# A decode block's load queue in written order, its row loads moved and cut, its last weight loads cut finer, and fewer warm matmuls

## The chip, the cores and the metric

The kernel runs on one core of one Trainium2 chip. The metric is device time in microseconds (us) of one execution. A profiled execution has a span (first to last instruction), and its own time is a little longer.

The engines are TensorE (PE; its weight loads are listed as PEld), VectorE (DVE), ScalarE (ACT), GpSimd (POOL) and SyncE (SP). SyncE and ScalarE each have a DMA queue here. All DMAs run on the core's 16 DMA engines.

## What is computed

A pre-norm attention block with a KV cache, one token for each of 4 batch entries, then a channel MLP. All data are float32.

```python
x = A_x                                             # (4, 1, 448)
y = layernorm(x)
q = (y @ wq)                                        # 16 heads of 256
k, v = last 1024 positions of the caches            # 8 kv heads, 2 q heads each
p = softmax(q k^T * 256 ** -0.5);  o = p v
h = x + o @ wo
z = layernorm(layernorm(h))
out = h + gelu(z @ w1 + b1) @ w2 + b2               # 448 -> 1792 -> 448
```

The caches, cut to their last 1024 positions, and the weights are 88 MB, each byte read once.

## The kernel before

**Groups.** The 8 kv heads are 8 groups, numbered 0 to 7. For each group the kernel projects `q` (`project_q`: matmuls `pq`, a copy `qs` on ScalarE, four transposes `pqt`, DVE work into `qT`), computes scores in two halves of 512 positions (`scores_half`: 8 matmuls `s`, a maximum `mx` on DVE), the softmax (`softmax`: DVE's `nm`, two exponentials `p` on ScalarE, row sums and `rec`), transposes the exponentials (`transpose_p`: `ppt`, then DVE copies into `pT`), multiplies with the values (`values`: 16 matmuls into `po`), and adds the group's output (`finish`: DVE's `o`, transposes `pot`, DVE's `oT`, matmuls `acc` with the group's `wo`). Four matmuls with 32 rows each go to the four column groups of the TensorE array, one per batch entry or per quarter of the work.

**Loads.** Three big buffers of the pool `ring` are filled in turn (`slot`). The first, `t`, gets `wq` for group 0, the keys of group 0 (`k0`) and part of `wq` for group 1; the rest of that comes by two small transfers into `wq1_last`. Then each load is one DMA of 7,040 or 7,936 KB: `ta`, `tb`, `tc`, `td` for g = 0, and again for g = 3, which bring keys, values and weights of three groups packed by the host in the order of their use. The end (`te0` to `te2`, one in each of the three buffers) holds the keys of group 7, values and `wo` of groups 6 and 7, and the MLP weights `w1` and `w2`, in 11 DMAs. A load into a buffer waits until the last reader of what was in it is done.

**Rows.** `rs` holds three row blocks that the MLP part at the end needs: `xb` (the input), `b2b` and `b1b` (biases), four partitions for each quarter of the array. GpSimd clears it, and ScalarE issues four DMAs (line 127) that fill it.

**Order.** TensorE runs in written order (`manual_schedule`); the other engines' instructions are put in order by a scheduler from the written one and the dependencies. DMAs on hardware queues take eight completion counters in turn; a DMA that takes one over waits until the DMA that had it before has landed.

**The end.** After the scores of group 7, `keep_warm` puts bf16 matmuls on a zero tile `idle` between TensorE's work: 2 ahead of `transpose_p` for group 7, 10 behind it, and one to three at later places. Then come the values of group 6 and 7, interleaved with the output of group 6; the sum `last` of all outputs in a layout of four quarters; the residual and two layer norms (`h`, `dh`, `z`, `pz`); `pu` (with `w1`), the GELU `u`, its transpose `put` into `gT`; and the second MLP product, of 14 chunks of 128 rows: `pa` takes chunks 0 to 7, is copied by ScalarE to `pas` and added in, and `py` takes chunks 8 to 13. DVE adds the residual (`res`) and SyncE stores it.

Of the kernel before, what the change touches and what calls it, by code (L numbers as in the profile page):

```python
# [15 lines left out]
B, D = 4, 448  # L16
# [4 lines left out]
P = 128  # L21
# [3 lines left out]
NFC = F // P  # L25
FQ = F // 4
Q = 32
CACHE = NKC * B * DH
# [7 lines left out]
def block_kernel(ctx: ExitStack, tc, rows, wq0, k0, wq1, la, lb, lc, ld, k7, vo, w1, w2, out):  # L36
    nc = tc.nc
# [12 lines left out]
    def slot(name):  # L50
        return ring.tile([P, SLOT], F32, tag="r", name=name)

    def load(t, at, src, pieces=None):
        dst = t[:, at : at + src.shape[-1]]
        at = 0
        for n in pieces or (src.shape[-1],):
            nc.sync.dma_start(dst[:, at : at + n], src[:, at : at + n])
            at += n
        return dst

    def cut(t, sizes):
        parts, at = [], 0
        for n in sizes:
            parts.append(t[:, at : at + n])
            at += n
        return parts


    def wq_parts(t, last=None):
        parts = [(a, yT[:, a, :], slice(0, 512), t[:, a * 512 : (a + 1) * 512]) for a in range(3)]  # L70
        if last is not None:
            return parts + [(3, yT[:H, 3, :], slice(0, 512), last)]
        for i in range(2):
            parts.append((3, yT[:, 3 + i, :], slice(i * 2 * P, (i + 1) * 2 * P), t[:, 3 * 512 :]))
        return parts


    def keys(t):
        return t.rearrange("p (c b k) -> p c b k", c=2, b=B)

    def chunks(t):
        v = t.rearrange("p (c b d) -> p c b d", b=B, d=DH)
        return [v[:, c : c + 2] for c in range(0, v.shape[1], 2)]
# [18 lines left out]
    yT = const.tile([P, ND + 1, Q], F32, name="yT")  # L102
# [20 lines left out]

    rs = const.tile([P, 2 * P + FQ], F32, name="rs")
    nc.gpsimd.memset(rs, 0.0)
    for j in range(4):
        nc.scalar.dma_start(rs[j * Q : j * Q + B, :], rows[j])
    xb, b2b, b1b = rs[:, :P], rs[:, P : 2 * P], rs[:, 2 * P :]


# [20 lines left out]
    def project_q(g, parts):  # L151
        pq = ps_m.tile([P, 512], F32, tag="m", name=f"pq{g}")
        for j, y, cols, w in parts:
            nc.tensor.matmul(pq[j * Q : (j + 1) * Q, cols], y, w, start=True, stop=True)  # L154
        qs = work.tile([P, 512], F32, tag="qs", name=f"qs{g}")
        nc.scalar.copy(qs, pq)  # L156

        pt = ps_m.tile([P, 2 * REP, P], F32, tag="m", name=f"pqt{g}")
        for i in range(2 * REP):
            nc.tensor.transpose(pt[:, i, :], qs[:, i * P : (i + 1) * P], ident)  # L160
        sm = work.tile([P, 2 * REP, B], F32, tag="sm", name=f"sm{g}")
        nc.vector.tensor_reduce(  # L162
            sm, pt.rearrange("p i (j q) -> p i q j", j=4)[:, :, :B, :], axis=AX.X, op=ALU.add
        )

        src = sm.rearrange("p (r c) b -> p c b r", r=REP)
        for i in range(2):
            nc.vector.tensor_copy(qT[g % 2][:, :, :, i * REP : (i + 1) * REP], src)

    def scores_half(g, h, kt):  # L170
        s = ps_s.tile([P, 512], F32, tag="s", name=f"s{g}_{h}")
        for c in range(2):
            for b in range(B):
                nc.tensor.matmul(  # L174
                    s[b * Q : (b + 1) * Q, :], qT[g % 2][:, c, b, :], kt[:, c, b, :],
                    start=(c == 0), stop=(c == 1),
                )
        m = work.tile([P, 1], F32, tag=f"mx{h}", name=f"mx{g}_{h}")
        nc.vector.reduce_max(m, s, axis=AX.X)  # L179
        return s, m  # L180

    def softmax(g, parts):
        halves, mx = zip(*parts)
        nm = work.tile([P, 1], F32, tag="nm", name=f"nm{g}")
        nc.vector.tensor_max(nm, mx[0], mx[1])
        nc.vector.tensor_scalar_mul(nm, nm, -SCALE)  # L186
        p = once.tile([P, 2 * 512], F32, tag="p", name=f"p{g}")
        sums = work.tile([P, 2], F32, tag="sums", name=f"sums{g}")
        for h in range(2):
            nc.scalar.activation(  # L190
                p[:, h * 512 : (h + 1) * 512], halves[h], AF.Exp, bias=nm, scale=SCALE,
                accum_out=sums[:, h : h + 1],
            )
        rec = work.tile([P, 1], F32, tag=f"rec{g % 3}", name=f"rec{g}")
        nc.vector.tensor_add(rec, sums[:, 0:1], sums[:, 1:2])
        nc.vector.reciprocal(rec, rec)
        return p, rec

    def scores(g, kt):
        return softmax(g, [scores_half(g, h, kt[h]) for h in range(2)])  # L200

    def transpose_p(g, p):
        for h in range(2):
            pt = ps_t.tile([P, 4, P], F32, tag="t", name=f"ppt{g}_{h}")
            for c in range(4):
                nc.tensor.transpose(pt[:, c, :], p[:, (4 * h + c) * P : (4 * h + c + 1) * P], ident)  # L206

            src = pt.rearrange("p (c i) (b q) -> p c i b q", i=2, b=B)
            for i in range(2):
                nc.vector.tensor_copy(  # L210
                    pT[g % 2][:, 2 * h : 2 * h + 2, :, i * REP : (i + 1) * REP], src[:, :, i, :, :REP]
                )


    def values(g, vt, po, pairs=range(NKC // 2)):
        for c in pairs:
            for b in range(B):
                nc.tensor.matmul(  # L218
                    po[b * Q : (b + 1) * Q], pT[g % 2][:, c, b, :], vt[c][:, :, b, :],
                    start=(c == 0), stop=(c == NKC // 2 - 1),  # L220
                )
# [35 lines left out]
    def po_tile(g, pool=ps_o, tag="o"):  # L257
        return pool.tile([P, 2, DH], F32, tag=tag, name=f"po{g}")
# [6 lines left out]
    ka, kb, wqt1 = cut(load(t, WEIGHTS + ND * B, k0), (HALF, HALF, 3 * 512))  # L265
# [12 lines left out]
    nc.vector.tensor_mul(yT[H:, 4, :B], d[H:, 3, :], rx[H:, :])  # L278
    project_q(0, wqt)

    p, rec = scores(0, [keys(ka), keys(kb)])
    project_q(1, wq_parts(wqt1, wq1_last))
    transpose_p(0, p)

    def finish(g, po, rec, wt):
        transposed_output(g, po, rec)
        add_output(g, output_weights(wt))

    for g in (0, 3):
        ka, kb, wqt, va = cut(load(slot(f"ta{g}"), 0, la[g // 3]), (HALF, HALF, WEIGHTS, HALF))  # L290
        p, rec_next = scores(g + 1, [keys(ka), keys(kb)])
        project_q(g + 2, wq_parts(wqt))
        transpose_p(g + 1, p)
        po = po_tile(g)
        va = chunks(va)
        values(g, va, po, range(0, 2))

        vb, wot, ka, kb = cut(load(slot(f"tb{g}"), 0, lb[g // 3]), (HALF, WEIGHTS, HALF, HALF))
        values(g, va + chunks(vb), po, range(2, 4))
        p, rec_then = scores(g + 2, [keys(ka), keys(kb)])  # L300
        finish(g, po, rec, wot)
        transpose_p(g + 2, p)

        wqt, v, wot, ka = cut(load(slot(f"tc{g}"), 0, lc[g // 3]), (WEIGHTS, CACHE, WEIGHTS, HALF))
        project_q(g + 3, wq_parts(wqt))
        po = po_tile(g + 1)
        values(g + 1, chunks(v), po)
        first_half = scores_half(g + 3, 0, keys(ka))
        finish(g + 1, po, rec_next, wot)

        kb, wqt, v, wot = cut(load(slot(f"td{g}"), 0, ld[g // 3]), (HALF, WEIGHTS, CACHE, WEIGHTS))
        p, rec = softmax(g + 3, [first_half, scores_half(g + 3, 1, keys(kb))])
        project_q(g + 4, wq_parts(wqt))
        transpose_p(g + 3, p)
        po = po_tile(g + 2)
        values(g + 2, chunks(v), po)
        finish(g + 2, po, rec_then, wot)


    g = HKV - 2  # L320
    e = [slot(f"te{i}") for i in range(3)]
    kt = [keys(t) for t in cut(load(e[0], 0, k7), (HALF, HALF))]
# [2 lines left out]
    vt_last = chunks(load(e[2], 0, vo[1][:, :CACHE], (CACHE // 4, CACHE // 2, CACHE // 4)))  # L325
    wo_last = output_weights(load(e[1], CACHE + WEIGHTS, vo[1][:, CACHE:]))
    w1t = cut(load(e[0], CACHE, w1, (2 * F, F + F // 2)), (F, F, F, F // 2))
    w2t = cut(load(e[2], CACHE, w2, (8 * D, 4 * D, 2 * D)), NFC * (D,))
    p, rec_last = scores(g + 1, kt)


    warm0 = ps_o.tile([P, 512], F32, tag="o", name="warm0")

    def keep_warm(n, warm):
        for _ in range(n):
            nc.tensor.matmul(warm[:Q], idle[:, :Q], idle, start=True, stop=True)  # L336

    keep_warm(2, warm0)
    transpose_p(g + 1, p)
    keep_warm(10, warm0)  # L340
    po = po_tile(g)
    values(g, vt, po)
    po_last = po_tile(g + 1, ps_t, "t")
# [17 lines left out]
    for i in range(4):  # L361
        for j in range(4):
            nc.tensor.matmul(
                ph[j * Q : (j + 1) * Q], oT[(g + 1) % 2][:, i, :], columns(wo_last[:, i, :], j),
                start=False, stop=(i == 3),
# [18 lines left out]
    h = once.tile([P, P], F32, tag="h", name="h")  # L384
# [27 lines left out]
    for a in range(ND):  # L412
        m = Q if a == 0 else B
        for j in range(4):
            rows, w = w1_part(a, j)
# [31 lines left out]
    for c in range(first):  # L447
        j, m = c % 4, Q if c < 4 else B
# [6 lines left out]
    for c in range(first, NFC):  # L455
        for j in range(4):
            m, n = (Q, 2) if c == first else (B, 2 if j < 3 else 1)
# [80 lines left out]
```

## Time and profile before

| | us |
|---|---|
| median of 3 executions | 215.76 |
| lowest, highest of the 3 | 214.77, 216.06 |
| profiled execution: its own time | 214.81 |
| its span | 213.0 |

In the profile's 40 slices each digit is a busy share in tenths. A row of the chain of waits has a start, a length and what the time went to; "x16" counts instructions. In a row of instruction groups, "out<-in" are the program's names without numbers, and a matmul on float32 data leaves two records. A bracket at the end of a timeline row gives the idle time of the engine before the row and what ended it. The mean granted clock of TensorE was 0.848 of full speed.

### The profile page before, as it was taken

How to read it: one execution, taken by the hardware profiler on the slowest of the kernel's cores; microseconds unless marked ns; L12 is line 12 of the kernel's file. 1: busy time of each engine (PE TensorE's matmuls, PEld its weight loads, DVE VectorE, ACT ScalarE, POOL GpSimd, SP SyncE). 2: the span in 40 equal slices, each digit the busy share in tenths (PEclk: the TensorE clock that was granted, in tenths of full speed). 3: DMA queues.
4: the chain of work that ended last, by engine and by line, in shares of the span. 5: the costliest groups of instructions: out<-in, count | busy, mean ns of one | idle time of the engine just before them, and what ended most of it. 6: DMA issues, size and time to landing. Idle time of an engine off the chain costs nothing.

```text
span 213.0 us, 2294 instructions
## 1 busy us (share of the span) xinstructions
PE 137.4 (64%) x971; PEld 48.2 (23%) x971; DVE 38.4 (18%) x167; ACT 21.2 (10%) x52; POOL 5.6 (3%) x17
## 2 busy tenths in 40 slices
PE   0456824872970595289398198239809876998993
PEld 0322211220220221023123022113202322334432
DVE  1420320320230012012114013100301223122320
ACT  0210110120020100021003001000000302000310
POOL 6100000000000000000000000000000000000110
PEclk9999995796697579769859959955965999999999
DMA  7999899999999999999999999999999998999990
GB/s 291 433 392 502 381 486 391 447 467 409 417 453 444 417 417 477 390 465 391 458 423 444 425 456 417 429 417 465 405 410 415 430 450 380 435 414 435 420 376 34
DMA packets 3289, 88.46 MB, mean 415 GB/s; under 512 B 384, under 2 KB 512, under 8 KB 1104
## 3 DMA queue, kind: packets, MB, share of 16 engines
q1 hardware_dynamic: 3248, 88.29, 96.7%
q8 instruction: 7, 0.11, 0.2%
q10 hardware_dynamic: 32, 0.05, 0.1%
q14 instruction: 2, 0.02, 0.0%
HBM read 88.26 MB, written 0.07 MB: 415 GB/s over the span
## 4 chain that ended last, share of the span: by engine, by line
DMA 64%; PE 29%; DVE 3%; ACT 1%; issue 1%; SPq 0%; ACTq 0%; DVEq 0%
DMA ta<-la 21%; DMA td<-ld 20%; DMA tb<-lb 16%; PE s L174 8%; DMA t<-k 8%; PE po L218 8%; PE ppt L206 2%; PE pu L416 2%; PE warm L336 1%; PE acc L247 1%; PE pq L154 1%; PE pot L239 1%; PE pa L449 1%; DVE o L235 1%; DVE mx L179 1%
## 5 line engine op out<-in xcount | busy, mean ns | idle before, releaser
L179 DVE TENSOR_REDUCE mx<-s 128x1 f32<-128x512 f32 x16 | 11.1, 691 | 61.0 <-PE s L174 61.0
L174 PE MATMUL s<-ta,qT 128*32 128x512 f32 x64 | 12.2, 935 | 8.9 <-DMA ta<-la 8.9
L156 ACT COPY qs<-pq 128x512 f32<-128x512 f32 x8 | 4.7, 585 | 112.3 <-PE pq L154 112.3
L190 ACT ACTIVATE p<-s,nm 128x512 f32<-128x512 f32 x16 | 10.9, 687 | 45.9 <-DVE nm L186 45.9
L174 PE MATMUL s<-td,qT 128*32 128x512 f32 x32 | 7.3, 1061 | 12.0 <-DMA td<-ld 12.0
L235 DVE TENSOR_SCALAR o<-po,rec 128x512 f32<-128x512 f32 x8 | 6.0, 751 | 47.1 <-PE po L218 47.1
L218 PE MATMUL po<-tb,pT 128*32 128x512 f32 x32 | 7.3, 1061 | 10.4 <-DMA tb<-lb 10.4
L154 PE MATMUL pq<-tc,yT 128*32 128x512 f32 (+1 forms) x20 | 3.9, 890 | 14.8 <-DMA tc<-lc 14.8
L206 PE MATMUL ppt<-ident,p 128*128 128x128 f32 x64 | 10.5, 286 | 2.0 <-ACT p L190 1.7
L218 PE MATMUL po<-tc,pT 128*32 128x512 f32 x64 | 10.5, 815 | 0.0
L160 PE MATMUL pqt<-ident,qs 128*128 128x128 f32 x32 | 6.6, 341 | 6.0 <-ACT qs L156 6.0
L174 PE MATMUL s<-tb,qT 128*32 128x512 f32 x64 | 9.1, 717 | 0.0
L206 PEld LDWEIGHTS ppt<-ident,p 128*128 128x128 f32 x64 | 6.7, 140 | 7.1 <-ACT p L190 7.1
L218 PE MATMUL po<-te,pT 128*32 128x512 f32 x64 | 7.9, 596 | 0.1
L162 DVE TENSOR_REDUCE sm<-pqt 128x16 f32<-128x64 f32 x8 | 1.8, 224 | 33.9 <-PE pqt L160 33.9
L174 PE MATMUL s<-t,qT 128*32 128x512 f32 x32 | 6.1, 925 | 2.6 <-DMA t<-k 2.6
L218 PE MATMUL po<-td,pT 128*32 128x512 f32 x64 | 7.3, 595 | 0.0
L336 PE MATMUL warm<-idle 128*32 128x512 bf16 x25 | 7.3, 382 | 0.0
L160 PEld LDWEIGHTS pqt<-ident,qs 128*128 128x128 f32 x32 | 4.2, 169 | 12.1 <-ACT qs L156 10.3
L174 PEld LDWEIGHTS s<-ta,qT 128*32 128x32 f32 x64 | 2.9, 163 | 17.4 <-issue 14.4
L239 PE MATMUL pot<-ident,o 128*128 128x128 f32 x32 | 5.2, 287 | 2.2 <-DVE o L235 2.2
L148 POOL TENSOR_TENSOR r<-ve_r,mhalf 128x1 f32<-128x1 f32 x2 | 1.1, 542 | 192.2 <-DVE ve_r L147 192.2
(129 smaller groups left out, 113.4 us busy)
## 6 DMA issues: line engine op xcount, KB each, us to landing
tc<-lc SPq DMA_DIRECT2D x2, 7936.0 KB
td<-ld SPq DMA_DIRECT2D x2, 7936.0 KB
ta<-la SPq DMA_DIRECT2D x2, 7040.0 KB, 29.4
tb<-lb SPq DMA_DIRECT2D x2, 7040.0 KB, 34.3
te<-vo SPq DMA_DIRECT2D x1, 4992.0 KB, 27.2
t<-k SPq DMA_DIRECT2D x1, 4864.0 KB, 16.4
te<-k SPq DMA_DIRECT2D x1, 4096.0 KB, 36.9
te<-w SPq DMA_DIRECT2D x2, 1792.0 KB, 28.0
```

Source lines behind the costliest of these rows:

```text
L154: nc.tensor.matmul(pq[j * Q : (j + 1) * Q, cols], y, w, start=True, stop=True)
L156: nc.scalar.copy(qs, pq)
L160: nc.tensor.transpose(pt[:, i, :], qs[:, i * P : (i + 1) * P], ident)
L174: nc.tensor.matmul(s[b * Q : (b + 1) * Q, :], qT[g % 2][:, c, b, :], kt[:, c, b, :], start=(c == 0), stop=(c == 1),)
L179: nc.vector.reduce_max(m, s, axis=AX.X)
L190: nc.scalar.activation(p[:, h * 512 : (h + 1) * 512], halves[h], AF.Exp, bias=nm, scale=SCALE, accum_out=sums[:, h : h + 1],)
L206: nc.tensor.transpose(pt[:, c, :], p[:, (4 * h + c) * P : (4 * h + c + 1) * P], ident)
L218: nc.tensor.matmul(po[b * Q : (b + 1) * Q], pT[g % 2][:, c, b, :], vt[c][:, :, b, :], start=(c == 0), stop=(c == NKC // 2 - 1),)
L235: nc.vector.tensor_scalar_mul(o, po, rec)
L239: nc.tensor.transpose(pt[:, i, c], o[:, i, c * P : (c + 1) * P], ident)
L336: nc.tensor.matmul(warm[:Q], idle[:, :Q], idle, start=True, stop=True)
L416: nc.tensor.matmul(pu[j * Q : j * Q + m, :], zT[rows, a, :m], w, start=(a == 0), stop=(a == ND - 1),)
```

## The change

Four things are changed.

1. SyncE and ScalarE are added to the engines that run in written order. So that ScalarE's written order suits, `scores` no longer contains the softmax; it is called where wanted, behind the next group's `project_q`.
2. The four row transfers at the start are taken out. Rows are loaded by seven: four behind the load of `tb` for g = 0 (two quarters, each cut into columns 0 to 255 and 256 to 703), three behind that of `td` (one quarter cut the same way, one whole).
3. The last weights `w2` come in loads of 8, 3, 2 and 1 chunks, where it was 8, 4 and 2.
4. Around `transpose_p` of group 7, the 2 and 10 warm matmuls become two `fill` matmuls (float32, on real data, output unused) and 2 warm ones.

```diff
-    for j in range(4):
-        nc.scalar.dma_start(rs[j * Q : j * Q + B, :], rows[j])
...
     def scores(g, kt):
-        return softmax(g, [scores_half(g, h, kt[h]) for h in range(2)])
+        return [scores_half(g, h, kt[h]) for h in range(2)]
...
-        p, rec_next = scores(g + 1, [keys(ka), keys(kb)])
+        parts = scores(g + 1, [keys(ka), keys(kb)])
         project_q(g + 2, wq_parts(wqt))
+        p, rec_next = softmax(g + 1, parts)
         transpose_p(g + 1, p)
...
         vb, wot, ka, kb = cut(load(slot(f"tb{g}"), 0, lb[g // 3]), (HALF, WEIGHTS, HALF, HALF))
+        if g == 0:
+            for j in range(2):
+                for cols in (slice(0, 2 * P), slice(2 * P, 2 * P + FQ)):
+                    nc.scalar.dma_start(rs[j * Q : j * Q + B, cols], rows[j][:, cols])
...
         kb, wqt, v, wot = cut(load(slot(f"td{g}"), 0, ld[g // 3]), (HALF, WEIGHTS, CACHE, WEIGHTS))
-        p, rec = softmax(g + 3, [first_half, scores_half(g + 3, 1, keys(kb))])
+        if g == 0:
+            for j in range(2, 4):
+                for cols in ((slice(0, 2 * P), slice(2 * P, 2 * P + FQ)) if j < 3 else (slice(0, 2 * P + FQ),)):
+                    nc.scalar.dma_start(rs[j * Q : j * Q + B, cols], rows[j][:, cols])
+        parts = [first_half, scores_half(g + 3, 1, keys(kb))]
         project_q(g + 4, wq_parts(wqt))
+        p, rec = softmax(g + 3, parts)
...
-    w2t = cut(load(e[2], CACHE, w2, (8 * D, 4 * D, 2 * D)), NFC * (D,))
-    p, rec_last = scores(g + 1, kt)
+    w2t = cut(load(e[2], CACHE, w2, (8 * D, 3 * D, 2 * D, D)), NFC * (D,))
+    p, rec_last = softmax(g + 1, scores(g + 1, kt))
...
+    def fill(n):
+        for _ in range(n):
+            nc.tensor.matmul(warm0[:Q], yT[:, 0, :], kt[0][:, 0, 0, :], start=True, stop=True)
+
+    fill(2)
+    transpose_p(g + 1, p)
     keep_warm(2, warm0)
-    transpose_p(g + 1, p)
-    keep_warm(10, warm0)
...
-        with tc.manual_schedule(engines={mybir.EngineType.PE}):
+        with tc.manual_schedule(engines={mybir.EngineType.PE, mybir.EngineType.SP, mybir.EngineType.Activation}):
```

SyncE's queue at the start, before. `t`, `ta`, `tb`, `tc` are the first buffers, `wq`, `k`, `la`, `lb`, `lc` their inputs; the bracket names what the DMA waits for, DMAHWn being completion counter n.

```order
L57 DMA t_134<-wq 128x1808
L57 DMA t_134<-k 128x9728
L267 DMA wq_last<-wq 32x1x512 x2
L57 DMA ta_239<-la 128x14080 [waits DMAHW0_49]
L57 DMA tb_313<-lb 128x14080 [waits DMAHW1_49]
L57 DMA tc_382<-lc 128x15872 [waits DMAHW2_49,DVE_49,PE_49]
```

The same place in the changed kernel.

```order
L57 DMA t_130<-wq 128x1808
L57 DMA t_130<-k 128x9728
L265 DMA wq_last<-wq 32x1x512 x2
L57 DMA ta_235<-la 128x14080
L57 DMA tb_309<-lb 128x14080
L57 DMA tc_382<-lc 128x15872 [waits DMAHW1_49,DMAHW0_49,DMAHW2_49,DVE_49,PE_49]
```

The loads stand in the same sequence; the waits of the first `ta` and `tb` for the counters of `wq` and `k` are gone.

ScalarE's queue in the changed kernel, from the exponentials of group 1 (`p_279`) to those of group 2 (`p_348`).

```order
L188 ACTIVATE p_279,sums_280<-s_0_237,nm_276 128x512 [waits DVE_49,Activation_49]
L188 ACTIVATE p_279,sums_280<-s_1_248,nm_276 128x512
L302 DMA rs<-rows 4x256 [waits Pool_49]
L302 DMA rs<-rows 4x448
L302 DMA rs<-rows 4x256 [waits DMAHW0_49]
L302 DMA rs<-rows 4x448 [waits DMAHW1_49]
L188 ACTIVATE p_348,sums_349<-s_0_323,nm_345 128x512 [waits DVE_49,PE_49,Activation_49]
```

Before, the four row transfers stood ahead of everything on ScalarE. The other three now stand between the copies `qs` of groups 3 and 4.

TensorE around the last scores, before: `s_1` is the second half of the scores of group 7, `warm` what `keep_warm` writes, `ppt` the transposes of group 7's exponentials, `po_886` the values of group 6. Of the warm matmuls one is shown at each of the two places.

```order
L174 MATMUL s_1_838<-te_813,qT_112 32x512 x8
L336 LDWEIGHTS idle
L336 MATMUL warm_859<-idle 32x512
...
L206 MATMUL ppt_0_862<-ident,p_852 128x128 x4
L206 MATMUL ppt_1_869<-ident,p_852 128x128 x4
...
L218 MATMUL po_886<-te_814,pT_113 32x512 x16
```

The same place in the changed kernel, with the first of two warm matmuls.

```order
L172 MATMUL s_1_842<-te_816,qT_112 32x512 x8
L349 MATMUL warm_863<-te_816,yT 32x512 x2
L204 MATMUL ppt_0_866<-ident,p_856 128x128 x4
L204 MATMUL ppt_1_873<-ident,p_856 128x128 x4
L345 LDWEIGHTS idle
L345 MATMUL warm_863<-idle 32x512
...
L216 MATMUL po_882<-te_817,pT_113 32x512 x16
```

Two `fill` matmuls stand ahead of the transposes, and between the transposes and `po` there are 2 warm matmuls instead of 10.

More of the change, by code (lines that the diff above doesn't have):

```diff
@@ L279, in block_kernel @@
     project_q(0, wqt)
-    p, rec = scores(0, [keys(ka), keys(kb)])
+    parts = scores(0, [keys(ka), keys(kb)])
     project_q(1, wq_parts(wqt1, wq1_last))
+    p, rec = softmax(0, parts)
     transpose_p(0, p)
@@ L298, in block_kernel @@
         vb, wot, ka, kb = cut(load(slot(f"tb{g}"), 0, lb[g // 3]), (HALF, WEIGHTS, HALF, HALF))
+        if g == 0:
+            for j in range(2):
+                for cols in (slice(0, 2 * P), slice(2 * P, 2 * P + FQ)):
+                    nc.scalar.dma_start(rs[j * Q : j * Q + B, cols], rows[j][:, cols])
         values(g, va + chunks(vb), po, range(2, 4))
-        p, rec_then = scores(g + 2, [keys(ka), keys(kb)])
+        p, rec_then = softmax(g + 2, scores(g + 2, [keys(ka), keys(kb)]))
         finish(g, po, rec, wot)
```

## The prediction

> **What bounds the kernel now.** I read the profile's page first, for engine shares and the DMA row, and took the chain of waits next.
>
> ```profile
> PE 137.4 (64%) x971; PEld 48.2 (23%) x971; DVE 38.4 (18%) x167; ACT 21.2 (10%) x52; POOL 5.6 (3%) x17
> DMA  7999899999999999999999999999999998999990
> q1 hardware_dynamic: 3248, 88.29, 96.7%
> q10 hardware_dynamic: 32, 0.05, 0.1%
> ```
>
> The DMA engines are busy in all but the first and the last slice; no compute engine is. q1 is SyncE's queue, q10 ScalarE's, which carries only the `rs` rows. Next the chain that ended last (start, length, what).
>
> ```profile
> 17.56 34.27 DMA tb<-lb
> ...
> 61.75 44.26 DMA ta<-la
> ...
> 117.86 42.28 DMA td<-ld
> ...
> 160.19 3.64 PE s L174 x16
> ...
> 181.65 2.27 PE warm L336 x10
> ...
> 183.97 4.50 PE po L218 x40
> ...
> 206.29 1.75 PE pa L449 x16
> ...
> 208.12 0.54 ACT pas L453
> ...
> 209.12 0.92 PE py L459 x11
> ...
> 210.07 0.29 DVE res L465
> ```
>
> The second `ta` lands at 61.75 + 44.26 = 106.01 and the second `td` at 117.86 + 42.28 = 160.14. After 160.14 the chain holds no DMA: it is TensorE with DVE and ACT between, and ten matmuls on zeros (`warm`) stand in it for 2.27 us. So the program is a load stream up to 160, then a race between the rest of that stream and a compute chain. How near the two are, the DMA issues tell (size of one, us to landing).
>
> ```profile
> tc<-lc SPq DMA_DIRECT2D x2, 7936.0 KB
> td<-ld SPq DMA_DIRECT2D x2, 7936.0 KB
> tb<-lb SPq DMA_DIRECT2D x2, 7040.0 KB, 34.3
> te<-vo SPq DMA_DIRECT2D x1, 4992.0 KB, 27.2
> te<-k SPq DMA_DIRECT2D x1, 4096.0 KB, 36.9
> te<-w SPq DMA_DIRECT2D x2, 1792.0 KB, 28.0
> te<-vo SPq DMA_DIRECT2D x2, 1024.0 KB
> te<-vo SPq DMA_DIRECT2D x1, 2048.0 KB
> te<-w SPq DMA_DIRECT2D x1, 1344.0 KB
> t<-wq SPq DMA_DIRECT2D x1, 904.0 KB, 4.6
> te<-vo SPq DMA_DIRECT2D x1, 896.0 KB
> te<-w SPq DMA_DIRECT2D x1, 896.0 KB, 26.1
> te<-w SPq DMA_DIRECT2D x1, 448.0 KB
> ```
>
> Between 106.01 and 160.14 `tb`, `tc` and `td` land: 22,912 KB in 54.13 us, 423 KB/us. After 160.14 all the `te` loads are left, 20,352 KB, which at that rate end at 208.2. The compute chain reaches the last weight chunks in 209.12 to 210.04. The stream thus ends some 1 to 1.5 us ahead of what uses it: TensorE sets the end, but with a slack of about one microsecond behind it.
>
> **The change part by part.** *Written order for SyncE and ScalarE, and the rows behind the first loads.* In SyncE's rows above, the loads stand in the same sequence before and after, so the written order by itself moves nothing. Only the counter waits of the first `ta` and `tb` go, as the four `rs` transfers no longer use up the counters ahead of them.
>
> ```profile
> SPq L57 <- PE acc L247: 75.0, 6, 14.7
> SPq L57 <- DMA t<-k: 11.9, 1, 11.9
> SPq L466 <- DMA te<-vo: 4.6, 1, 4.6
> ```
>
> SyncE waited 11.9 us for `k` and then issued `tb` at 17.56; now it issues it about 14 us sooner. I cost this at nothing: at 17.56 `ta` still had 7,040 KB to move (16.6 us at 423 KB/us), and DMA is busy in every slice there, so `tb` only queues longer. From `tc` on SyncE waits for a buffer that TensorE has to leave (the 75.0 us), which no part of the change touches. Without that cover the gain would be up to 14 us (a rival).
>
> The rows now go out from ScalarE in two places. The first four stand between the exponentials of groups 1 and 2; the counters waited for are those of `wq` and `k`, long landed by then. Behind them is queued the exponential of group 2, and TensorE's transposes wait for that.
>
> ```profile
> 4.07 1.54 ACTq L127 DMA_DIRECT2D rs<-rows  x4
> ...
> 60.89 0.69 ACT L190 ACTIVATE p<-s,nm 128x512 f32<-128x512 f32 x1 [17.08 <-DVE nm L186]
> ...
> 94.68 0.58 ACT L156 COPY qs<-pq 128x512 f32<-128x512 f32 x1 [21.41 <-PE pq L154]
> ```
>
> Four issues take 1.54 us and ScalarE is idle for 17.08 us there; the other three stand behind the copy of `qs` for group 3, in the 21.41 us before that for group 4, and the counters that they take are those of the first `ta` and `tb`, landed by 52, and of the first row transfer. Cost nothing. `rs` is first read at the end (`h`, after 196). The transfers themselves cost stream time: 0.1% of 16 engines over 213 us is 3.4 engine-us for four, at least 0.2 us of stream (spread over 16), at most 0.85 (on four engines, if each of the four partitions of a transfer goes by one). Seven for the same bytes add between 0 (by bytes) and 3/4 of 0.85 = 0.64 us. I take 0.1, near the byte end, since the rows are as long in all.
>
> The softmax calls written behind `project_q` leave TensorE's, DVE's and ScalarE's sequence as it was. Nothing.
>
> *The warm matmuls.* Two float32 fillers replace two bf16 ones ahead of the transposes, and eight of ten bf16 ones behind them are gone.
>
> ```profile
> L57 SPq DMA_DIRECT2D te<-w x5: 328/432/442, 176.7 to 184.2; - x5
> ...
> 174.62 3.62 PE L174 MATMUL s<-te,qT 128*32 128x512 f32 x32
> 180.32 1.32 PE L206 MATMUL ppt<-ident,p 128*128 128x128 f32 x8 [1.68 <-ACT p L190]
> ```
>
> The 16 score matmuls (two records each) take 3.62 us, four abreast, so one alone takes between 0.23 (if not abreast) and 0.9. I take 0.9: two end at 178.24 + 1.8 = 180.05, within the 1.68 us that TensorE waits for ScalarE before 180.32, with 0.3 to spare. Cost nothing; at half clock it would be 1.5.
>
> Eight warm matmuls less at 2.27/10 each save 1.8 us: `po` can start at 181.65 + 0.45 = 182.1 instead of 183.97. Its values (4,992 KB, issued at 154.46) land at 154.46 + 27.2 = 181.66, just in time. Saved so far 1.87 us. Now what is late next. From 181.66 at 423 KB/us the rest lands as follows: second `vo` piece 188.9 (189.2 by SyncE's waits: behind the last issue, 184.2 + 0.4, the store's counter waits 4.6 us for it), third 191.3, `w1` 197.7 and 200.9, first `w2` piece 205.1. The last is better read from its own time to landing: third of the `te<-w` issues (first at 176.7, some 0.43 each), near 177.5, and 28.0 later, 205.5; the other load of 1,792 KB was in use by 199.6. Moving the chain 1.87 forward, TensorE wants the second `vo` piece at 189.0 (waits 0.2), the third at 190.9 (waits 0.5 to 0.7), the second half of `w1` at 200.9 (about even), and `pa` wants the first `w2` piece at 205.4; it gets it at 205.5 to 205.6. `pa` thus starts 0.7 us sooner than at 206.29, and the fixed steps behind it (`pa`, `pas`, `py`) end 0.7 sooner, `res` at 209.35.
>
> *w2 in 8, 3, 2, 1.* Does the end of the stream allow 209.35?
>
> ```profile
> 207.83 0.35 PEld L459 LDWEIGHTS py<-te,gT 128*32 128x32 f32 x16 [0.65 <-DMA te<-w]
> ```
>
> Before, the second `w2` piece landed at 207.83, where 10,816 KB from 181.66 give 207.2: 0.6 late over eight transfers, under 0.1 each. Now three chunks (672 KB) come at 206.7 + 0.6 = 207.3, so chunks 8 to 10 no longer wait, two more at 208.3, and the last at 208.3 to 208.9 plus 0.1 for one transfer more. One chunk then needs a quarter of 0.92 us: `res` at 208.6 to 209.3. Stream and compute now end together, near 209.3 to 209.5.
>
> The fixed part of a transfer, by the trace: `t<-wq`, 904 KB, took 4.6 us to land where the rate gives 2.1, so 2.5 lie around it. [...]
>
> **The sum.** The profiled execution took 214.81 us, span 213.0 and 1.8 around it. Minus 0.7, plus 0.1: 214.2. The three others took 214.77, 215.76 and 216.06, median 215.76. Taken from the median the sum gives 215.15. Why two of them are longer no row shows; if it is compute behind 160, the new slack takes part of it up. I put the median halfway, at 214.7.
>
> **The rivals.**
> - *The stream is already the end* (nothing gained). If the seven row transfers add 0.64 us of stream, and the last `w2` piece costs as much as it saves, `res` stays at 210. For it: DMA at 9 in nearly every slice. Against it: chunks 12 and 13 did not wait. Time 215.0 to 216.0.
> - *More than 0.7.* If the pieces land by the plain rate (`w2` at 205.1, end 208.3), the cap is near 208.9 instead of 210.07, 1.2 less: 213.6 from the profiled execution.
> - *The clock falls* (slower). The place is behind the transposes, where eight warm matmuls are gone.
>
> ```profile
> 116.00:120.00 4.00, 1.80 (x16) 0.29 (x12) 0.24 (x2) 0.00 (x0) 0.00 (x0) 1.00 0.94 408
> 120.00:124.00 4.00, 1.31 (x8) 0.40 (x12) 0.00 (x0) 0.00 (x0) 0.00 (x0) 0.70 1.06 457
> ...
> 176.00:180.00 4.00, 2.64 (x26) 0.62 (x18) 1.70 (x4) 0.51 (x1) 0.00 (x0) 1.00 0.96 412
> ```
>
> In these windows (length, busy time of TensorE first, granted clock third from the end) TensorE is busy for the first 1.80 us of the first and the last 1.31 of the second, idle from 117.8 to 122.7, and the clock of the second is 0.70: half speed from about 121.6, after 3.8 us of idling. The 1.68 us before 180.32 left it at 1.00, as the third window shows. So it decides at a gap between 1.7 and 3.8 us; the largest that I foresee is 0.7. If it fell, the 16 records of 160.19 show the price: 3.64 us where 32 took 3.62 at full clock. `po` at half clock costs 4.5 us more, 2.6 beyond the 1.87 saved: 217.4 from the profiled execution, 218.4 from the median. [...]
> - *Small transfers in line* (slower): three more row transfers and one more of `w2`, each holding up the stream by the 2.5 us around `t<-wq`, 10 us: 225. Against it the 0.6 us over eight.
> - *The freed `tb` helps* (faster): the chain goes through `tb<-lb`, 34.27 us, and if its early issue let it land sooner, the end would come sooner by up to the 14 us of its issue. Against it: the busy DMA and the fixed bytes. 201 to 213.
>
> **How the numbers follow.** Forecast 0.60, stream already the end 0.18, more than 0.7 0.12, clock 0.06, transfers in line 0.02, `tb` 0.02. The range takes in the first three: 213.5 (the cap, from the profiled execution) to 216.1 (no gain, the highest time). About 1% is what a measurement of this kernel tells from no change, 213.6 to 217.9. Faster: `tb`, half of "more", and 0.06 of the forecast for the spread of the runs, 0.14. Slower: clock, transfers, 0.02 for chance, 0.10. Within: 0.76.
>
> **What would show it.** `po` of group 6 starts near 182.1; TensorE then waits for `te<-vo` and `te<-w`, which it hardly does now; the last `td` still lands 160 us in; `tb` is issued before 5 us and lands near 52 all the same; the clock is 1.00 from 168 on. The prediction is wrong if the second `td` lands more than 1 us away from 160, if a stretch behind 182 shows a clock under 1, or if the last `w2` piece lands after 209.5.

## The result and the profile after

| us | before | changed |
|---|---|---|
| median (6 executions each) | 215.86 | 214.11 |
| lowest, highest | 214.77, 216.17 | 213.97, 214.17 |
| profiled execution, its span | 214.81, 213.0 | 214.17, 212.4 |

The ratio is 0.9938, with a 95% interval from 0.9916 to 0.9961. It is a small gain that the interval keeps clear of 1, inside the forecast range. Two things are gained at once: the lowest time comes down by 0.8 us, and the spread shrinks from 1.4 us to 0.2. The size of the gain in the median, 1.75 us, owes something to the six executions of before, of which five took over 215.2; against 21 executions of before in a later job (median 215.01) the changed kernel's 214.09 is 0.9 us less, ratio 0.9963 (0.9937 to 0.9989).

The page of the changed kernel, the same rows as were shown of before:

```profile
PE 138.0 (65%) x965; PEld 47.7 (22%) x965; DVE 38.4 (18%) x167; ACT 21.2 (10%) x52; POOL 5.6 (3%) x17
DMA  7999898989999999989999999998989989999991
q1 hardware_dynamic: 3392, 88.29, 97.0%
q10 hardware_dynamic: 56, 0.05, 0.1%
```

The stream is as full as it was. The rows' queue now has 56 packets for the same bytes. The chain of waits of the changed kernel (start, length, what):

```profile
3.71 47.92 DMA tb<-lb
...
61.66 44.35 DMA ta<-la
...
117.87 42.29 DMA td<-ld
...
177.69 28.09 DMA te<-w
...
205.92 1.75 PE pa L462 x16
...
207.74 0.54 ACT pas L466
...
208.75 0.92 PE py L472 x11
...
209.69 0.29 DVE res L478
```

The first `tb` is issued 13.9 us sooner and lands at 51.63 where it landed at 51.83; the second `td` lands at 160.16 where it landed at 160.14. Up to there nothing has changed. Behind it the warm matmuls are no longer in the chain; the first load of `w2` is, and `res` starts at 209.69 instead of 210.07. What TensorE waits for in between, in the timeline of the changed kernel (the bracket is idle time and its cause):

```profile
182.24 4.50 PE L216 MATMUL po<-te,pT 128*32 128x512 f32 x40
...
189.12 0.16 PEld L216 LDWEIGHTS po<-te,pT 128*32 128x32 f32 x8 [0.36 <-DMA te<-vo]
...
191.60 1.07 PE L216 MATMUL po<-te,pT 128*32 128x512 f32 x8 [0.34 <-DMA te<-vo]
...
201.31 1.80 PE L429 MATMUL pu<-te,zT 128*4 128x448 f32 x16 [0.42 <-DMA te<-w]
...
205.92 1.71 PE L462 MATMUL pa<-te,gT 128*32 128x448 f32 x16 [0.30 <-DMA te<-w]
```

The values of group 6 start 1.73 us sooner (183.97 before). Then four loads in turn take the lead away: 1.15 is left at the third `vo` piece (192.75 before), 0.71 at the second half of `w1` (202.02 before), 0.37 at `pa`.

### The profile page after: what moved, and what is told of

Same layout as the page of the kernel before. It is cut to its first block, busy times and chain, and to the rows that moved or that the text cites. A ratio compares the mean times of both kernels' runs of the same rounds, so it can differ in the third digit from the quotient of the medians.

```text
span 212.4 us, 2289 instructions
## 1 busy us (share of the span) xinstructions
PE 138.0 (65%) x965; PEld 47.7 (22%) x965; DVE 38.4 (18%) x167; ACT 21.2 (10%) x52; POOL 5.6 (3%) x17
## 3 DMA queue, kind: packets, MB, share of 16 engines
q1 hardware_dynamic: 3392, 88.29, 97.0%
## 4 chain that ended last, share of the span: by engine, by line
DMA 77%; PE 17%; SPq 2%; DVE 1%; ACT 1%; issue 1%; ACTq 0%
DMA tb<-lb 23%; DMA ta<-la 21%; DMA td<-ld 20%; DMA te<-w 13%; PE s L172 7%; PE po L216 4%; SPq L57 2%; PE pq L152 1%; PE ppt L204 1%; PE acc L245 1%; PE pa L462 1%; SPq L265 1%; PE pqt L158 1%; ACT qs L154 1%; PE py L472 0%
## 5 line engine op out<-in xcount | busy, mean ns | idle before, releaser
L172 PE MATMUL s<-ta,qT 128*32 128x512 f32 x64 | 12.7, 966 | 8.1 <-DMA ta<-la 8.1
L172 PEld LDWEIGHTS s<-ta,qT 128*32 128x32 f32 x64 | 3.0, 168 | 16.8 <-issue 13.9
L208 DVE COPY pT<-ppt 128x16 f32<-128x16 f32 x32 | 4.7, 171 | 7.6 <-PE ppt L204 7.6
```

What stands on the lines that cost most here:

```text
L172: nc.tensor.matmul(s[b * Q : (b + 1) * Q, :], qT[g % 2][:, c, b, :], kt[:, c, b, :], start=(c == 0), stop=(c == 1),)
L208: nc.vector.tensor_copy(pT[g % 2][:, 2 * h : 2 * h + 2, :, i * REP : (i + 1) * REP], src[:, :, i, :, :REP])
```

## The experiments

All ratios are to the kernel before, run on the same chip in the same job. Over the three jobs it took 214.5 to 216.3, with 34 of 79 executions above 215.2; one of 248.54, which nothing here explains, is among them. Its median was 215.01, 215.03 and 215.04 in the three, so that times of different jobs, though on different chips, may be set side by side to about 0.1 us.

### The parts, one at a time

**Only the edit around the last transposes**, put into the kernel before (with `fill` defined as in the changed kernel):

```diff
-    keep_warm(2, warm0)
+    fill(2)
     transpose_p(g + 1, p)
-    keep_warm(10, warm0)
+    keep_warm(2, warm0)
```

> The kernel before with the one edit around the last transposes (two float32 fillers ahead, two warm matmuls behind instead of ten). Theory A (the gain is the 1.8 us of warm matmuls, capped by the landing of the w2 pieces): first values of group 6 start near 182.2, the second w2 piece is waited for longer than the 0.65 us of before, res near 209.7 to 209.9, time 0.4 to 0.6% under before, spread as narrow as that of the changed kernel (0.2 us). Theory B (the gain is the early issue of tb and the rows' move): no change, 0.998 to 1.002. Theory C (the w2 cut carries it): at most 0.2% gained.

Measured: median 214.49, 214.34 to 214.65 in 12 executions, ratio 0.9964 (0.9950 to 0.9979). The mechanism and the narrow spread (0.3 us) are as theory A has them; the gain, 0.36%, lies just under the 0.4 to 0.6 that it expected. In the profile `py` waits for `w2` up to 207.90 and `res` starts at 209.74.

**Everything but that edit** (the changed kernel with `keep_warm(2)`, transposes, `keep_warm(10)`):

> The changed kernel with the old warm matmuls (2 and 10) put back. Theory A: first values of group 6 at 183.9, res at 210.0, time as before, ratio 0.998 to 1.002, and the wide spread of before (1.4 us) is back. Theory B: as fast as the changed kernel, ratio 0.992 to 0.996, narrow spread. Theory C: half of the gain stays, ratio near 0.997.

Measured: median 214.69, 214.42 to 216.04, five of 12 executions above 215.2; ratio 0.9998 (0.9977 to 1.0019). The chain of waits of this kernel:

```profile
181.68 2.28 PE warm L345 x10
...
210.09 0.29 DVE res L478
```

The early `tb`, the moved rows and the finer `w2` together leave `res` where it was (210.07). B and C fall. That the spread of before is back is as A expected.

**The changed kernel with `w2` in 8, 4 and 2 chunks:**

```diff
-    w2t = cut(load(e[2], CACHE, w2, (8 * D, 3 * D, 2 * D, D)), NFC * (D,))
+    w2t = cut(load(e[2], CACHE, w2, (8 * D, 4 * D, 2 * D)), NFC * (D,))
```

> The changed kernel with w2 in 8, 4 and 2 chunks. Theory A: chunk 8 then waits for four chunks, to about 207.8 instead of 207.4, but the sum of the first eight is copied only by 208.3, so res moves by 0.1 to 0.4 us at most: ratio 0.994 to 0.996 against before. Theory C: the gain is gone, ratio near 1.

Measured: 214.26, ratio 0.9958 (0.9943 to 0.9973), against 214.09 for the changed kernel in another job. The chain of this kernel:

```profile
207.78 0.64 PE py L472 x13
...
209.58 0.29 DVE res L478
```

Chunk 8 waits until 207.78, and `res` is no later for it. What the finer cut brings is 0.2 us at most.

**The rows back at the start** (the changed kernel with the four transfers of before, ahead of everything on ScalarE):

> The changed kernel with the four row transfers back at the start, ahead of everything on ScalarE, so that ta and tb wait for their counters as before. If the rows and the early issue of tb are worth nothing: 214.0 to 214.3, that of the changed kernel. If they are worth what the two single-edit kernels differ by (214.49 with the warm edit alone, 214.26 with all but the w2 cut): 214.3 to 214.5, with the last td or the w2 pieces 0.2 us later.

Measured: 214.34, 214.19 to 214.52, ratio 0.9961 (0.9947 to 0.9976): 0.25 us above the changed kernel's 214.09 in another job. The place that was expected is wrong, though. In its profile `res` starts at 209.70, as in the changed kernel; the difference lies behind the store. First this kernel's SyncE waits, then the changed kernel's:

```profile
SPq L539 <- DMA out<-res: 1.1, 1, 1.1
```

```profile
SPq L545 <- DMA out<-res: 0.9, 1, 0.9
```

From the start of `res` to the end of the span (which is given to 0.1 us), the kernels with rows at the start take 2.90 to 2.99 us (six profiles), those with the rows moved 2.65 to 2.72 (six profiles), and two with the rows moved and more `w2` loads 2.81 and 2.85. So the place of the rows alone does not decide it. By the kernels' instruction order the store takes completion counter 3 or 4 in the first group, 6 or 7 in the second, 0 and 1 in those two. Whether the counter is the cause was not tried.

### What holds the clock

**Neither fillers nor warm matmuls** around the last transposes, else the changed kernel:

```diff
-    fill(2)
     transpose_p(g + 1, p)
-    keep_warm(2, warm0)
```

> The changed kernel without the two fillers ahead of the last transposes and without the two warm matmuls behind them. Theory A: the values of group 6 start at about 181.7, but the second and third vo pieces and the w2 pieces still set the rest, so the time is that of the changed kernel within 0.1%. The rival that the clock falls when warm matmuls go: TensorE idles 2 us ahead of 180.3, the granted clock of the windows behind 180 falls under 1 and the time rises by 2 us or more, ratio above 1.003.

Measured: median 214.73, in two groups, six executions at 214.06 to 214.47 (mean granted clock 0.839 to 0.856) and six at 214.99 to 215.53 (0.824 to 0.832); ratio 0.9973 (0.9951 to 0.9994). The profiled one took 215.36. Its windows (length, busy time and count of PE, PEld, DVE, ACT, POOL, granted clock, DMA share, GB/s):

```profile
160.00:164.00 4.00, 3.73 (x21) 1.00 (x25) 0.03 (x1) 0.00 (x0) 0.00 (x0) 0.52 0.95 410
...
180.00:184.00 4.00, 3.00 (x19) 1.11 (x20) 0.69 (x6) 0.20 (x2) 0.00 (x0) 0.61 0.96 403
184.00:188.00 4.00, 4.00 (x24) 1.05 (x20) 0.00 (x0) 0.00 (x0) 0.00 (x0) 0.54 0.99 418
```

and its timeline:

```profile
179.58 1.33 PE L204 MATMUL ppt<-ident,p 128*128 128x128 f32 x8 [2.09 <-ACT p L188]
181.89 7.37 PE L216 MATMUL po<-te,pT 128*32 128x512 f32 x40 [0.98 <-DMA te<-vo]
```

The clock falls to half at 180.9, though TensorE never idles for more than 2.1 us at a stretch, and 20 value matmuls take 7.37 us instead of 4.50. Theory A was wrong on this kernel in half of its executions, and the rival's price (2 us or more) was too high: `res` starts at 210.85, 1.16 later than in the changed kernel, as the rest of the 2.87 us lies ahead of loads that are late anyway.

That raised a question on the kernel before: are its executions above 215.2 ones in which the clock falls too? Call it theory A2.

**Only the fillers**, in the kernel before (2 bf16 ahead become 2 float32; the ten behind stay):

> The kernel before with one edit: the two bf16 warm matmuls ahead of the last transposes become the two float32 fillers; the ten behind stay. Theory A2 (two separate gains: the fillers keep the clock from falling behind 180, which it does in some executions of before and costs those about 1 us; the eight warm matmuls less give the other 0.4): all times within 0.4 us of each other, near 214.6 (the low end of before), nothing over 215.2, ratio near 0.997. Rival (the spread of before has another source, the stream or the start): spread 1.4 us as before, ratio 0.999 to 1.001.

Measured: 214.36 to 215.10, none of 12 above 215.2; median 214.60, ratio 0.9977 (0.9960 to 0.9994). With seven of the 21 executions of before in that job above 215.2, the upper group is gone; a spread of 0.7 stays.

**The changed kernel with `keep_warm(2)` in place of `fill(2)`:**

> The changed kernel with the two fillers turned back into two bf16 warm matmuls. Theory A2: the low end is that of the changed kernel (214.0 to 214.2), but part of the executions, a third to a half, take 215 to 215.6; in a profiled one of these the granted clock is under 1 behind 180. Rival: all within 0.3 us, as the changed kernel.

Measured: 213.94 to 214.15 in 6 executions, median 214.07, ratio 0.9948 (0.9929 to 0.9968): A2's expectation missed. Yet the clock did fall in the profiled one, which took 213.99. Its windows, then its timeline and chain:

```profile
176.00:180.00 4.00, 2.32 (x18) 0.74 (x10) 1.33 (x4) 1.45 (x4) 0.00 (x0) 1.00 0.96 412
180.00:184.00 4.00, 3.86 (x19) 1.24 (x22) 0.70 (x6) 0.00 (x0) 0.00 (x0) 0.57 0.96 403
```

```profile
181.86 5.49 PE L216 MATMUL po<-te,pT 128*32 128x512 f32 x40
```

```profile
209.51 0.29 DVE res L478
```

A stretch at half clock costs 1 us at `po`, and `res` is not a bit later (209.69 in the changed kernel): the slack in front of the late loads takes it up. It is not that one execution alone: three of the six have a mean granted clock of 0.829 and three of 0.847, and they take 213.99 to 214.09 and 213.94 to 214.15. So in these six, with two warm matmuls ahead and two behind, the fillers are not needed for the time; with ten behind they are.

**The kernel before once more, profiled twice:**

> The kernel before, unchanged, for another profiled execution. It takes 214.5 to 215.1 in about six of ten executions and 215.2 to 216.3 in the rest. If the clock behind 180 makes the difference: an execution over 215.3 shows a granted clock under 1 in a window behind 180 (half for one window of some 3.4 us, 1 to 1.5 us of work lost) and res near 211, with the second td landing near 160 as ever; one under 215 shows 1.00 there. If the stream makes it: td lands about 1 us later in the long one, at a clock of 1.00 behind 168.

> The same again, for a second chance at a long execution; the two theories expect of it what they expect of the other.

The first took 214.82, with a clock of 1.00 throughout behind 168 and `res` at 210.09. The second took 215.44. Its windows and its chain:

```profile
160.00:164.00 4.00, 3.82 (x25) 1.08 (x26) 0.24 (x1) 0.00 (x0) 0.00 (x0) 0.57 0.95 410
...
180.00:181.00 1.00, 1.00 (x5) 0.55 (x6) 0.69 (x6) 0.00 (x0) 0.00 (x0) 0.74 0.67 279
...
183.00:184.00 1.00, 1.00 (x4) 0.34 (x3) 0.00 (x0) 0.00 (x0) 0.00 (x0) 0.56 0.95 401
```

```profile
160.18 3.50 PE s L174 x16
...
173.81 3.48 PE s L174 x32
...
180.71 3.86 PE warm L336 x10
184.61 4.50 PE po L218 x40
...
210.71 0.29 DVE res L465
```

The scores on the last `td` start at 160.18, as ever. The ten warm matmuls take 3.86 us instead of 2.27, as the clock is half from 180.48 to 183.88; `res` starts 0.64 later and the time is 0.63 longer. The loss at the warm matmuls is larger than that, 1.6 us: because the clock had risen sooner after 160, TensorE came to them 0.94 ahead (180.71 against 181.65). The theory of the clock holds in this execution; the stream is cleared of it.

### The price of more transfers

**The first `w2` load in two**, so 4, 4, 3, 2, 1:

> The changed kernel with the first w2 load of 8 chunks cut in two of 4, so w2 in 4, 4, 3, 2, 1. If the landing of the first eight chunks (205.9) is what holds pa: pa starts at 205.6, its second half waits till 205.9, the end comes 0.1 to 0.3 us sooner, 213.85 to 214.05. If each transfer adds to the stream: 0.1 us later.

**The changed kernel again**, in the same job:

> The changed kernel once more, on the same chip as the three others, to set them beside it. All theories: 213.9 to 214.3, spread under 0.4 us, ratio 0.992 to 0.997.

Measured: 214.23 (214.13 to 214.37) against 214.09 (seven executions at 214.02 to 214.38, one at 215.81, not explained); ratios 0.9959 and 0.9963. In the profile of the finer cut `pa` does start 0.1 us sooner, at 205.81, and so does `res`, at 209.59, but from there to the end it takes 2.81 us instead of 2.70, and the median is 0.14 higher. Nothing gained.

**`w2` in 14 loads of one chunk:**

> The changed kernel with w2 in 14 loads of one chunk (224 KB each) instead of four loads. If each transfer costs the stream under 0.1 us: 0.3 to 1 us longer, 214.4 to 215.1. If each stood in line with the 2.5 us seen around the first load: 25 us longer. If they are free: 213.8 to 214.1, as pa can then start with the first four chunks.

Measured: 214.73 (214.67 to 214.91), 0.64 above the changed kernel; ratio 0.9975 (0.9961 to 0.9990). Its chain of waits:

```profile
205.54 4.20 DMA te<-w
209.73 0.04 issue
209.78 0.45 PE py L472 x2
...
210.25 0.29 DVE res L478
```

The last chunk now lands at 209.73 and is waited for. Ten transfers more move `res` from 209.69 to 210.25, 0.06 us each; the last packet ahead of the store moves from 208.4 to 209.2, 0.08 each, as the changed kernel had some room behind it. Whether the price is one of the transfers or of their smaller packets (4,832 on SyncE's queue instead of 3,392) is not separated. In this stream, where the DMA engines are 0.8 or more busy in each of the 40 slices but the first and the last, the price of one transfer more is thus 0.06 to 0.08 us, and not the 2.5 us that lie around the bytes of the first load (`t<-wq`, 4.6 us to landing before).

## Why the prediction was right, and where it was off

The mechanism came as forecast, and none of the three signs that the prediction named for being wrong appeared: the second `td` lands at 160.16, the clock is 1.00 behind 182, and the last packet of `w2` is through at 208.4. Several sizes were off.

- **Early `tb`, written order, softmax moved: nothing.** Right. `tb` and `td` land where they did, and all but the warm edit gives 0.9998.
- **1.87 us saved by the warm matmuls, then late loads.** Right in mechanism; 1.73 came off at `po`. The sum said 0.7 at `res`, the profiles show 0.38. Mis-sized were two landings. The second half of `w1` was put at 200.9, "about even"; it came 0.4 later. There the rate of 423 KB/us was applied without the 0.3 to 0.6 us that the landings seen (189.2, 207.83) lay behind it. The first `w2` piece was put at 205.5, from an issue near 177.5 and 28.0 to landing; the issue was done at 177.69, the load landed 28.09 later, at 205.78, and `pa` started at 205.92.
- **Rows: 0.1 us of stream more.** Not seen: the second `td` lands at 160.16 (160.14 before), and with everything but the warm edit `res` stays at 210.09. What there is lies elsewhere and has the other sign: the kernels with moved rows end 0.2 us sooner behind the store. With `res` 0.38 sooner that makes the 0.6 of the spans. This step was not foreseen at all, and its cause stays open. That the sum's 214.2 for the profiled execution met the measured 214.17 is luck: the 0.3 too much that it took off at `res` is made up by the 0.1 of stream that did not come and the 0.2 behind the store.
- **`w2` in 8, 3, 2, 1: the end of the stream allows it.** Right: the finer cut is worth 0.2 us at most, and without it `res` stood no later.
- **The median halfway between the profiled execution and the median of before: 214.7.** This was the step that was off most: 214.11. I argued that slack would take up "part" of the longer executions if they were compute behind 160. They are, at least where a trace shows one (215.44), and in the changed kernel nothing is left of it: the sum from the profiled execution alone gives 214.2, 0.1 from the measured median, though by the luck just named.
- **The clock rival.** Its chance was small because I read "1.68 us left it at 1.00" as a bound for the gap. One execution was no evidence for that: in another the same gap of 1.68 us, with transposes behind it, ended at half clock. The changed kernel kept its time for two reasons. With the fillers the clock stays up (1.00 behind 166 in both of its profiles), and the slack takes up a fall that costs 1 us at `po`; without fillers and warm matmuls the fall costs 2.87, and the slack is not enough.

The time of a fall is not random within what the traces show. In the second profile of before the clock rises at 163.44 (0.57 in 160 to 164), falls at 180.48 and rises at 183.88: 17.04 = 5 x 3.41 and 3.40. In the kernel with no fillers it rises at 163.84, falls at 180.88 and rises again at about 187.7: 17.04 and 6.8 = 2 x 3.4. In the trace of the first profile of before the clock is 1.00 or 0.50, and the 15 stretches between its changes from 33 to 166 are 6.83 or 10.24 us long, 2 and 3 times 3.41; the trace of the changed kernel has the same stretches. So the changes seen here lie on a grid of 3.41 us, whose phase differs between executions (the rises at 163.44 and, below, at 165.92 lie 2.48 apart). On the phase of 163.44 one window of the grid runs from 177.09 to 180.50: of TensorE's work it holds the last 0.2 us of scores, two bf16 warm matmuls and 1.1 us of transposes, and the clock falls. On that of the first profile of before:

```profile
160.00:164.00 4.00, 3.81 (x20) 0.99 (x24) 0.10 (x1) 0.00 (x0) 0.00 (x0) 0.50 0.91 393
164.00:168.00 4.00, 3.24 (x22) 1.59 (x14) 1.75 (x10) 1.93 (x5) 0.00 (x0) 0.76 1.10 465
```

it rises at 165.92, the windows run from 176.16 and 179.57, the first holds 2.1 us of scores, the second 1.3 us of transposes and 1.3 of warm matmuls, and nothing falls. The other traces sort in the same way. Of the six profiles of kernels without fillers, the three in which the clock rises at 163.4 to 163.8 fall at 180.5 to 180.9, and the three in which it rises at 165.6 to 166.0 do not fall. Of the eight with fillers none falls, though in six of them the clock rises at 163.0 to 163.9. The second profile of the changed kernel is one of these six:

```profile
160.00:164.00 4.00, 3.81 (x25) 1.09 (x26) 0.26 (x1) 0.00 (x0) 0.00 (x0) 0.58 0.93 401
...
180.00:184.00 4.00, 3.36 (x28) 1.36 (x32) 0.69 (x6) 0.00 (x0) 0.00 (x0) 1.00 0.96 403
```

So in these 14 profiles the clock falls where the early phase and the thin window come together, and with the fillers there is no fall. TensorE is busy for 1.7 us of the window from 177.09, which lost the clock, and for 2.3 us of one that kept it (everything but the warm edit, 179.29 to 182.70). That the busy time of a window decides is my reading of them; no run here tests it alone.

That every execution of before above 215.2 is such a fall is not shown; one was profiled. The mean granted clock that is on record for each speaks for part of them: of the 33 from 215.2 to 216.4, 21 have 0.841 or less, and of the 45 below only one. The other 12 have 0.848 or more, and ten of them are among the twelve longest (from 215.84 on); the changed kernel's 215.81 has 0.847. What lengthens those stays open.

## What to carry to other kernels

Where a compute chain runs beside a load stream, work taken out of the chain is worth only its lead over the next loads (here 1.73 us at `po` became 0.38 at `res`): list their landings from the bytes and the rate, add what the landings seen lie behind that, and subtract at each one. A median that lies well above the lowest time is a second case to explain: profile it again until an execution of the upper group is caught, and lay the grid of clock changes over the chain. Slack behind a fragile stretch can stand in for work that keeps the clock up, as far as it reaches: here for a fall that cost 1 us, not for one that cost 2.9.

## What the hardware showed that was not expected

- The granted clock changed on a grid of 3.41 us: the stretches between changes in the traces of before and of the changed kernel are 6.83 or 10.24 us long up to 166. A window with 0.2 us of score matmuls, two bf16 warm matmuls and 1.1 us of transposes lost it; one with 2.1 us of score matmuls did not. In the second profile of the changed kernel the clock rises early too (0.58 in the window from 160), and with the fillers, which take 1.88 us of the thin window, it stays at 1.00.
- With `w2` in 14 loads, ten transfers more, of 224 KB each, cost 0.06 to 0.08 us apiece in a stream that keeps the DMA engines 0.8 or more busy, where the first load of the program shows 2.5 us around its bytes.
- The same store ends the span 2.7 to 3.0 us behind `res`, in groups that go with the completion counter that it takes, and so with the number of DMAs before it.
